# Seven half products in place of eight for the MLP input of two token blocks

## The chip, the cores and the metric

The kernel runs on one core of one Trainium2 chip. The metric is the device time of one execution in microseconds (us). Matmuls run on TensorE (PE in the profile), elementwise work on VectorE (DVE), ScalarE (ACT) and GpSimd (POOL); SyncE (SP) issues the transfers.

## The reference

Linear attention over 4 batches, 8 heads and 576 positions gives x of 2304 tokens by 512. A gated unit (GLU) and an MLP follow, both with float64 weights in memory and float32 results:

```
xn = x / rms(x) * rms_g
x2 = (silu(xn @ w_gate) * (xn @ w_val)) @ w_out      # 512 -> 1536 -> 512
h  = x2 @ w_in                                       # 512 -> 2048
out = silu(h) @ w_out2                               # 2048 -> 512
```

## The kernel before

Tokens are cut into five blocks: blocks 0 to 3 have 512 tokens, block 4 has 256. The 2048 MLP features are cut into 16 f groups of 128. Each float32 operand is kept as a high part (rounded to fp32r) and a low part (the rest), and each product is three matmuls: high by high, high by low, low by high (`PASS`).

For a block and an f group the input product (`part`, L250) is 12 matmuls: 4 chunks of 128 input features by 3 passes. ScalarE applies SiLU (L284) and makes the high part of h (L243), VectorE makes the low part (L244). The output product (`g2_mlp`, L337) takes all f groups of a sweep: for each tile of 128 tokens, 3 matmuls for each f group into one PSUM bank of the pool `ps_y`, which VectorE then adds to the block's sum in SBUF (L348; in the first sweep ScalarE copies, L346).

The MLP goes in six sweeps over all tokens, of 3, 3, 3, 3, 2 and 2 f groups. The order of the work is the order in which the code emits it, engine by engine. `stream` walks sweeps and blocks. A block's output product is not emitted at once: it waits in `pend` and is emitted after the SiLU and the split of a later input product, so that other matmuls lie between a SiLU and the products that read its result.

Weights of the next sweep are prepared in between. `stream` yields the PE time of each step; when W_PACE (5.5 us) or W_RUSH (3.2) has come together, `prep.tick` emits one step for up to three weights: the load (SP), the decode of the float64 words (five VectorE instructions, L154 to L165, then two GpSimd additions, L168), the high part (ACT, L191) and the low part (DVE, L194). Each engine works through its own queue in this order.

In the GLU the last sweep (two f groups) leaves each block's result in `ya` and splits it into `xs` (L317, L294), the MLP's input.

Of the kernel before, what the change touches and what calls it, by code (L numbers as in the profile page):

```python
# [20 lines left out]
def kernel(  # L21
# [99 lines left out]
    def wrows(w, f):  # L121
        return w.bitcast(U32)[f * P:(f + 1) * P, :]
# [139 lines left out]
    def g1_glu(f, j, hs, mid):  # L262
        prep.need((1, "g", f))
        p = ps_tile("ps_g", [P, blocks[j]])
        yield from proj(wt[1, "g", f], j, p)
        s = pools["s"][0].tile([P, blocks[j]], F32, tag="s", name="s", bufs=pools["s"][1])
        nc.scalar.activation(out=s, in_=p, func=AF.Silu)  # L267
        if blocks[j] == TB * P:
            yield from mid
        prep.need((1, "v", f))  # L270
        p = ps_tile("ps_g", [P, blocks[j]])
        yield from proj(wt[1, "v", f], j, p)
        nc.vector.tensor_tensor(out=s, in0=s, in1=p, op=ALU.mult)  # L273
        hs[f] = split_h(s, j)
        if blocks[j] < TB * P:
            yield from mid

    def g1_mlp(f, j, hs, mid, late):
        prep.need((2, "i", f))
        p = ps_tile("ps_g", [P, blocks[j]])  # L280
        yield from proj(wt[2, "i", f], j, p)
        yield from late
        s = pools["s"][0].tile([P, blocks[j]], F32, tag="s", name="s", bufs=pools["s"][1])
        nc.scalar.activation(out=s, in_=p, func=AF.Silu)  # L284
        hs[f] = split_h(s, j)
        yield from mid

    def g2_glu(fs, j, hs, first, last):
        prep.need(*[(1, "o", f) for f in fs])
        y = ya[j].rearrange("p (c t) -> p c t", c=KC)  # L290
        nn = 3 * len(fs)

        def low(d):
            nc.vector.tensor_tensor(  # L294
                out=xs[j][:, 1, d, :], in0=y[:, d, :],
                in1=xs[j][:, 0, d, :].bitcast(F32), op=ALU.subtract,
            )
# [57 lines left out]
    n2 = len(sweeps) - 1  # L355

    def stream():
        pend = ()
        prepped = 1
        for si, (kind, fs, side) in enumerate(sweeps):  # L360
            for j in range(NB) if si < n2 else [*range(NE), *range(NB - 1, NE - 1, -1)]:
                if si == 0 and j < NE:
                    continue
                hs = {}
                end = si == n2 and j == NE
                for f in fs:
                    if kind == 1:
                        yield from g1_glu(f, j, hs, pend)
                        pend = ()
                    else:  # L370
                        short = blocks[j] < TB * P
                        keep = f == fs[0] and (end or short)
                        mid, late_mid = ((), pend) if short else (pend, ())
                        yield from g1_mlp(f, j, hs, *(((), ()) if keep else (mid, late_mid)))
                        if not keep:
                            pend = ()
                    if si and prepped == si and si + 1 < len(sweeps):
                        prep.jobs += prep_list(si + 1)
                        prepped += 1
                if kind == 1:  # L380
                    pend = g2_glu(fs, j, hs, si == 0, si == n1)
                else:
                    pend = g2_mlp(fs, j, hs, si == n1 + 1, si == n2, end)
        yield from pend
# [699 lines left out]
    with tc.manual_schedule():  # L1084
# [105 lines left out]
```

## Time and profile before

| | us |
|---|---|
| median of 3 runs (lowest to highest) | 971.16 (970.67 to 972.09) |
| the profiled execution, and its span | 969.33, 967.5 |
| PE busy over the span | 961.1 (99%) |
| DVE, ACT, POOL busy | 558.1 (58%), 385.9 (40%), 292.1 (30%) |
| chain that ended last, PE's share | 97% |
| L250, input products: busy, count | 467.9, 2256 |
| L337, MLP output products: busy, count | 200.8, 870 |

The MLP takes the span from about 575 us to the end. A row of a timeline gives the start of a piece of work and how long it took; the bracket tells how long its engine had been idle, and what ended that.

### The profile page before, as it was taken

What the parts mean: (1) busy time and instruction counts of PE and PEld (TensorE: products, weight loads), DVE (VectorE), ACT (ScalarE), POOL (GpSimd) and SP (SyncE); (2) the same over time, 40 slices, a digit from 0 to 9 for tenths busy, and PEclk for the clock granted to TensorE, in tenths of its full rate; (3) what the DMA queues carried; (4) which work ended last, traced back from release to release, by engine and by line L of the source; (5) the groups of instructions that cost most, each with busy time, mean ns of one, the idle gap of its engine ahead of it and who ended that gap; (6) DMA issues with size and microseconds to landing.
All of it is one profiled execution on the core that took longest, in us unless ns stands there. A gap on an engine that the chain in (4) does not pass through costs nothing.

```text
span 967.5 us, 16801 instructions
## 1 busy us (share of the span) xinstructions
PE 961.1 (99%) x6658; PEld 807.8 (83%) x6658; DVE 558.1 (58%) x1163; ACT 385.9 (40%) x891; POOL 292.1 (30%) x308
## 2 busy tenths in 40 slices
PE   8999999999999999999999999999999999999998
PEld 6888888888889888888888888888888888888887
DVE  6998999685533466763326764515635635435634
ACT  6999886643211134331113344433223223222221
POOL 8888656253300133431002313403302402102200
PEclk9999999999999999999999999999999999999999
DMA  8655544122200012220000211201201201100023
GB/s 193 168 134 135 143 130 116 66 88 65 66 1 1 6 61 66 88 87 22 0 1 22 66 44 45 88 1 44 87 1 43 66 22 44 44 1 23 22 87 109
DMA packets 79486, 60.39 MB, mean 62 GB/s; under 512 B 27312, under 2 KB 73648, under 8 KB 79408
## 3 DMA queue, kind: packets, MB, share of 16 engines
q1 hardware_dynamic: 79136, 59.26, 21.2%
q8 instruction: 52, 0.85, 0.4%
q14 instruction: 26, 0.21, 0.1%
q10 hardware_dynamic: 272, 0.07, 0.0%
HBM read 49.87 MB, written 4.72 MB: 56 GB/s over the span
## 4 chain that ended last, share of the span: by engine, by line
PE 97%; DVE 1%; ACT 1%; issue 0%; DVEq 0%
PE g L250 47%; PE y L337 20%; PE y L304 13%; PE b L661 4%; PE b L250 4%; PE b L845 2%; PE kv L741 2%; PE b L1061 2%; PE b L634 2%; PE b L941 1%; PE b L821 1%; PE b L1102 0%; ACT e L710 0%; DVE small L678 0%; ACT m L176 0%; DVE m L154 0%
## 5 line engine op out<-in xcount | busy, mean ns | idle before, releaser
L250 PE MATMUL g<-xs,w 128*128 128x512 f32 (+1 forms) x2256 | 467.9, 366 | 0.0
L250 PEld LDWEIGHTS g<-xs,w 128*128 128x128 f32 x2256 | 391.1, 188 | 70.2
L168 POOL TENSOR_TENSOR m<-m,raw 128x512 int32<-128x512 int32 x136 | 188.5, 1386 | 581.3 <-issue 415.2
L244 DVE TENSOR_TENSOR h<-s,h 128x512 fp32r<-128x512 f32 (+1 forms) x134 | 96.0, 717 | 185.2 <-ACT h L243 185.2
L337 PE MATMUL y<-w,h 128*128 128x512 f32 (+1 forms) x870 | 200.8, 388 | 0.0
L337 PEld LDWEIGHTS y<-w,h 128*128 128x128 f32 x870 | 162.2, 188 | 33.3
L243 ACT ACTIVATE h<-s 128x512 fp32r<-128x512 f32 (+1 forms) x134 | 78.9, 589 | 182.0 <-DVE s L273 160.0
L304 PE MATMUL y<-h,w 128*128 128x512 f32 (+1 forms) x648 | 135.5, 366 | 0.2 <-DVE h L244 0.2
L304 PEld LDWEIGHTS y<-h,w 128*128 128x128 f32 x648 | 112.2, 189 | 20.2 <-DVE h L244 0.4
L284 ACT ACTIVATE s<-g 128x512 f32<-128x512 f32 (+1 forms) x80 | 44.5, 556 | 170.8 <-PE g L250 170.3
L348 DVE TENSOR_TENSOR ya<-y,ya 128x512 f32<-128x512 f32 (+1 forms) x91 | 62.2, 684 | 57.8 <-PE y L337 56.5
L315 DVE TENSOR_TENSOR ya<-y,ya 128x512 f32<-128x512 f32 (+1 forms) x80 | 50.4, 636 | 58.2 <-PE y L304 58.0
L273 DVE TENSOR_TENSOR s<-s,g 128x512 f32<-128x512 f32 (+1 forms) x54 | 33.9, 627 | 82.6 <-PE g L250 81.6
L710 ACT ACTIVATE e<-b,nb 128x128 f32<-128x128 f32 x272 | 76.2, 428 | 7.6 <-issue 4.4
L191 ACT ACTIVATE w<-m 128x512 fp32r<-128x512 f32 x68 | 43.3, 636 | 68.1 <-POOL m L168 67.6
L678 DVE TENSOR_REDUCE small<-b 128x4 f32<-128x512 f32 (+1 forms) x80 | 51.4, 643 | 6.5 <-PE b L661 2.7
L267 ACT ACTIVATE s<-g 128x512 f32<-128x512 f32 (+1 forms) x54 | 29.6, 548 | 59.9 <-PE g L250 59.8
L194 DVE TENSOR_TENSOR w<-m,w 128x512 fp32r<-128x512 f32 x68 | 51.2, 754 | 0.1
L587 POOL TENSOR_TENSOR sq<-sq 128x256 f32<-128x256 f32 (+1 forms) x80 | 45.4, 577 | 3.5
L661 PE MATMUL b<-om,hl 64*64 64x128 f32 x1152 | 41.9, 276 | 1.2 <-ACT hl L649 1.0
L583 POOL TENSOR_TENSOR sq<-x 128x512 f32<-128x512 f32 (+1 forms) x40 | 39.1, 980 | 12.9 <-DVE ns L596 4.7
L661 PEld LDWEIGHTS b<-om,hl 64*64 64x64 f32 x1152 | 32.1, 132 | 8.9 <-issue 3.6
(72 smaller groups left out, 703.7 us busy)
## 6 DMA issues: line engine op xcount, KB each, us to landing
raw<-in_moe_w_out_dram SPq DMA_DIRECT2D x28, 512.0 KB, 3.6
raw<-in_moe_w_in_dram SPq DMA_DIRECT2D x16, 512.0 KB, 3.7
raw<-in_moe_w_gate_dram SPq DMA_DIRECT2D x12, 512.0 KB, 3.7
raw<-in_moe_w_val_dram SPq DMA_DIRECT2D x12, 512.0 KB, 3.6
qT<-e SPq DMA_DIRECT2D x72, 64.0 KB, 2.6
x<-in_k_dram SPq DMA_DIRECT2D x16, 256.0 KB, 3.5
x<-in_q_dram SPq DMA_DIRECT2D x16, 256.0 KB, 3.3
va<-in_v_dram SPq DMA_DIRECT2D x32, 128.0 KB, 4.3
```

Of the source, the lines that this page charges most:

```text
L168: tt(out=mi, in0=mi, in1=(low if step == 5 else high).bitcast(I32), op=ALU.add)
L194: nc.vector.tensor_tensor(out=st.t[:, 1, :], in0=st.m.bitcast(F32), in1=st.t[:, 0, :].bitcast(F32), op=ALU.subtract)
L243: nc.scalar.activation(out=ht[:, 0, :], in_=s, func=AF.Copy)
L244: nc.vector.tensor_tensor(out=ht[:, 1, :], in0=s, in1=ht[:, 0, :].bitcast(F32), op=ALU.subtract)
L250: nc.tensor.matmul(out=ps, lhsT=w[:, a, cc * P:(cc + 1) * P], rhs=xs[j][:, c, cc, :], start=(n == 0), stop=(n == 3 * KC - 1),)
L304: nc.tensor.matmul(out=ps, lhsT=wt[1, "o", f][:, a, d * P:(d + 1) * P], rhs=hs[f][:, c, :], start=(n == 0), stop=(n == nn - 1),)
L315: nc.vector.tensor_tensor(out=y[:, d, :], in0=ps, in1=y[:, d, :], op=ALU.add)
L337: nc.tensor.matmul(out=ps, lhsT=hs[f][:, a, t * P:(t + 1) * P], rhs=wt[2, "p", f][:, c, d0:d1], start=(n == 0), stop=(n == nn - 1),)
L348: nc.vector.tensor_tensor(out=o[:, t, d0:d1], in0=ps, in1=o[:, t, d0:d1], op=ALU.add)
L661: nc.tensor.matmul(out=st.ps[e][cols, j, :], lhsT=st.xt[rows, j, cols], rhs=om2[rows, :], start=True, stop=True, skip_group_check=True,)
L678: nc.vector.tensor_reduce(out=st.mx.rearrange("p (j e) -> p e j", e=2)[:, e], in_=st.ps[e], axis=AX.X, op=ALU.max)
L710: nc.scalar.activation(out=st.e[r][:, :, h, :] if blocks4 else st.e[r][:, h, :], in_=src.rearrange("p (a f) -> p a f", a=4) if blocks4 els ...
```

## The change

For blocks 0 and 1 and a pair of f groups, the input product is a 2 by 2 product of halves: two blocks by two halves of the 512 input features (call block 0's halves a0 and b0, block 1's a1 and b1), times two feature halves by two f groups. It is eight half products of 6 matmuls. Strassen's scheme in Winograd's form needs seven, with sums of tokens and of weights as operands. All MLP sweeps now have two f groups, so there are eight.

- `token_sums`, once, at the end of the GLU: four subtractions of 128x1024 on GpSimd, in place in `ya` of blocks 0 and 1, and each result split into high (ACT) and low (DVE).
- `Mlp`, in place of `prep` for the MLP's weights: twelve jobs a sweep, one at a time, whenever M_PACE (3.6 us of PE) has come together. It adds two sums of weights for each sweep (four GpSimd instructions of 128x256, L444), and splits each (L426 on ACT, L430 on DVE).
- `quad`: the seven products P1 to P7 in four PSUM banks pa, pe, pb, pc. Partial sums pass from bank to bank by three ScalarE copies (L513), one of them, e, to SBUF; VectorE adds e to pb and later to pc (L525, `both`). pb is added to by P3, P5 and P6, and read in between. Between the products stand up to six tiles of the output product of blocks 3 and 4 of the sweep before (`more`), called Y1 to Y6 here. In the first sweep two matmuls initialise pb and pc.
- In blocks 2 and on the order is: input of block 2, first f, output of block 0; input of block 2, second f, output of block 1; then blocks 3 and 4.

```diff
-    for i, n in enumerate([3, 3, 3, 3, 2, 2]):
+    for i, n in enumerate([2] * (NF2 // 2)):
...
+        return [                                  # token_sums
+            lambda: less(a1, a1, a0),
+            lambda: (high(1, a1), less(b1, b1, a1)),
+            lambda: low(1, a1),
+            lambda: (high(2, b1), less(a0, b1, a0)),
...
+            self.jobs += [                        # Mlp.plan
+                (("load", s), lambda: load("i", 0)),
+                (("load", s), lambda: (dec("i", 0), load("i", 1))),
+                (("load", s), lambda: (hi("i", 0), dec("i", 1), load("p", 0))),
+                (("load", s), lambda: (lo("i", 0), hi("i", 1), load("p", 1))),
+                (("load", s), lambda: (lo("i", 1), sum12())),
+                (("s", s), lambda: (shi(0), sum34())),
+                (("s", s), lambda: slo(0)),
+                (("s2", s), lambda: (shi(1), dec("p", 0))),
+                (("s2", s), lambda: (slo(1), hi("p", 0))),
+                (("s2", s), lambda: (lo("p", 0), dec("p", 1))),
+                (("p", s), lambda: hi("p", 1)),
+                (("p", s), lambda: lo("p", 1)),
+            ]
...
+        product(w1, 0, half(0, 0), pa, True)      # quad: P1
+        copy(pb, pa)
+        yield from more()
...
+        product(s12, 0, summ(1), pe, True)        # P2
+        copy(e, pe)
+        yield from more()
+        yield step
+        product(s12, KH, summ(2), pb, False)      # P3
+        copy(pc, pb)
+        yield from more()
+        yield step
+        product(w1, KH, half(0, KH), pa, False)   # P4
+        t = silu(pa, s_tile())
+        yield from more()
+        hs[0][f1] = split_h(t, 0)
...
+        product(s34, 0, summ(3), pb, False)       # P5
+        t = both(pb)
+        yield from more()
+        hs[1][f2] = split_h(t, 1)
+        yield step
+        product(w2, KH, summ(4), pb, False)       # P6
+        t = silu(pb, s_tile())
+        yield from more()
...
+        product(s34, KH, half(1, KH), pc, False)  # P7
+        hs[1][f1] = split_h(both(pc), 1)
...
+            yield from quad(s, iter(pend), hs)    # stream
...
+            for n, f in enumerate(fs):
+                yield from g1_mlp(f, 2, hs[2], (), out_of(n, hs[n]))
...
+            elif due > M_PACE and mlp.tick():
                 due = 0.0
```

**Place 1: pb between P5 and P6, TensorE.** What TensorE does, before, in the second sweep (w0_0 to w0_2 are input weights; g is a PSUM bank of an input product, y one of an output tile, h the split result of a SiLU):

```order
L250 MATMUL g_7345<-xs0_90,w0_1_6987 128x512 x12
L250 MATMUL g_7365<-xs0_90,w0_2_7033 128x512 x12
L250 MATMUL g_7383<-xs1_91,w0_0_6910 128x512 x12
L337 MATMUL y_7401<-w0_3_7083,h_7320 128x512 [waits Activation_49]
L337 MATMUL y_7401<-w0_3_7083,h_7320 128x512
L337 MATMUL y_7401<-w0_3_7083,h_7320 128x512 [waits DVE_49]
```

In the changed kernel, third sweep (g_7485 is pb, y_7583 is Y5; w1_5 and w1_6, w1_7 and w1_8 hold token sums):

```order
L501 MATMUL g_7485<-w1_5_6531,w0_0_7503 128x512 [waits Activation_49]
L501 MATMUL g_7485<-w1_6_6532,w0_0_7503 128x512
L501 MATMUL g_7485<-w1_5_6531,w0_0_7503 128x512 [waits DVE_49]
L501 MATMUL g_7485<-w1_5_6531,w0_0_7503 128x512
L501 MATMUL g_7485<-w1_6_6532,w0_0_7503 128x512
L501 MATMUL g_7485<-w1_5_6531,w0_0_7503 128x512
L340 MATMUL y_7583<-w0_3_7142,h_7462 128x512 x3
L340 MATMUL y_7583<-w0_1_7226,h_7480 128x512 x3
L501 MATMUL g_7485<-w1_7_6556,w1_1_7361 128x512 [waits DVE_49]
L501 MATMUL g_7485<-w1_8_6557,w1_1_7361 128x512
L501 MATMUL g_7485<-w1_7_6556,w1_1_7361 128x512 x2
```

Before, the input products follow each other without a wait, each in a bank of its own. Now P6 adds to the bank of P5, and its first matmul waits for VectorE, with the six matmuls of Y5 between the two.

**The same place, VectorE.** What VectorE does, before, around a decode in the same sweep (ya0 is the sum of block 0):

```order
L348 TENSOR_TENSOR ya0_95<-y_7401,ya0_95 128x512
L154 TENSOR_SCALAR m0_7412<-raw0_7346 128x512
L157 TENSOR_SCALAR raw0_7346<-raw0_7346 128x512
L160 TENSOR_SCALAR m0_7412<-m0_7412 128x512
L162 TENSOR_SCALAR raw0_7346<-raw0_7346 128x512
L165 TENSOR_SCALAR m0_7412<-m0_7412 128x512
L348 TENSOR_TENSOR ya0_95<-y_7422,ya0_95 128x512
L348 TENSOR_TENSOR ya0_95<-y_7433,ya0_95 128x512
L348 TENSOR_TENSOR ya0_95<-y_7444,ya0_95 128x512
```

In the changed kernel, from the eviction of Y4 (y_7554) to that of Y5; m1 and raw1 are the decode of an output weight, w0_2 a weight that is split, s_7580 the sum of pb (g_7485) and e:

```order
L351 TENSOR_TENSOR ya3_3690<-y_7554,ya3_3690 128x512
L430 TENSOR_TENSOR w0_2_7529<-m0_7505,w0_2_7529 128x512
L154 TENSOR_SCALAR m1_7563<-raw1_7363 128x512
L157 TENSOR_SCALAR raw1_7363<-raw1_7363 128x512
L160 TENSOR_SCALAR m1_7563<-m1_7563 128x512
L162 TENSOR_SCALAR raw1_7363<-raw1_7363 128x512
L165 TENSOR_SCALAR m1_7563<-m1_7563 128x512
L244 TENSOR_TENSOR h_7571<-s_7552,h_7571 128x512
L525 TENSOR_TENSOR s_7580<-g_7485,e_7487 128x512
L351 TENSOR_TENSOR ya4_3691<-y_7583,ya4_3691 128x512
```

The eviction of Y4, the low part of one weight, the whole decode of the next and a split of h stand ahead of the addition L525 that reads pb. In sweeps 3 to 8 these rows are alike; in sweep 2 ScalarE evicts Y4, and in sweep 1 there is no Y5.

**Place 2: the second h of block 2, ScalarE.** What ScalarE does, before, where it makes two weights' high parts (L191):

```order
L191 ACTIVATE w1_4_7681<-m0_7613 128x512
L191 ACTIVATE w1_5_7715<-m1_7683 128x512
L284 ACTIVATE s_7729<-g_7713 128x512
L243 ACTIVATE h_7731<-s_7729 128x512
L284 ACTIVATE s_7747<-g_7734 128x512
L243 ACTIVATE h_7749<-s_7747 128x512
```

In the changed kernel, after the output of block 0 (w0_4 and w0_5 are the next sweep's input weights, s_7752 and h_7754 the second f group of block 2):

```order
L426 ACTIVATE w0_4_7711<-m0_7675 128x512
L426 ACTIVATE w0_5_7748<-m1_7713 128x512
L284 ACTIVATE s_7752<-g_7690 128x512
L243 ACTIVATE h_7754<-s_7752 128x512
L284 ACTIVATE s_7770<-g_7757 128x512
L243 ACTIVATE h_7772<-s_7770 128x512
```

Two high parts stand ahead of a SiLU in both. Before, TensorE has 12 matmuls of 512 columns, 24 of 256 and three more between that SiLU's product (g_7713) and the first matmul that reads h_7731. Now block 1's output product follows g_7690, the jobs that end in the two high parts are emitted within it, and from its end there are the 12 matmuls of g_7757 and three more up to the first that reads h_7754.

## Rows read from the trace of the kernel before

**Rows 1.** The page: busy time by engine, then the chain of waits by engine
```profile
PE 961.1 (99%) x6658; PEld 807.8 (83%) x6658; DVE 558.1 (58%) x1163; ACT 385.9 (40%) x891; POOL 292.1 (30%) x308
...
PE 97%; DVE 1%; ACT 1%; issue 0%; DVEq 0%
```

**Rows 2.** Busy time by stretch, in the MLP: us, PE, PEld, DVE, ACT, POOL, PEclk
```profile
700.00:760.00 60.00, 60.00 (x283) 50.36 (x282) 27.06 (x50) 16.47 (x29) 10.91 (x8) 1.00 0.11 34
...
577.00:968.00 391.00, 387.19 (x1805) 324.25 (x1803) 181.89 (x326) 115.74 (x202) 73.40 (x52) 1.00 0.14 45
```

**Rows 3.** Timeline of TensorE, MLP outputs: start us, us, engine line op out<-in xcount
```profile
852.02 6.32 PE L337 MATMUL y<-w,h 128*128 128x512 f32 x27
```

**Rows 4.** Timeline of VectorE, same stretch: evictions of these outputs
```profile
854.29 0.69 DVE L348 TENSOR_TENSOR ya<-y,ya 128x512 f32<-128x512 f32 x1 [2.20 <-PE y L337]
856.33 0.69 DVE L348 TENSOR_TENSOR ya<-y,ya 128x512 f32<-128x512 f32 x1 [1.35 <-PE y L337]
858.37 0.69 DVE L348 TENSOR_TENSOR ya<-y,ya 128x512 f32<-128x512 f32 x1 [1.35 <-PE y L337]
```

**Rows 5.** Timeline of VectorE, MLP: a decode and what follows it
```profile
897.12 0.42 DVE L165 TENSOR_SCALAR m<-m 128x512 uint32<-128x512 uint32 x1
897.46 0.69 DVE L244 TENSOR_TENSOR h<-s,h 128x512 fp32r<-128x512 f32 x1
898.06 1.28 DVE L348 TENSOR_TENSOR ya<-y,ya 128x512 f32<-128x512 f32 x2
...
901.31 0.69 DVE L348 TENSOR_TENSOR ya<-y,ya 128x512 f32<-128x512 f32 x1 [0.67 <-PE y L337]
901.91 0.68 DVE L194 TENSOR_TENSOR w<-m,w 128x512 fp32r<-128x512 f32 x1
902.63 0.43 DVE L154 TENSOR_SCALAR m<-raw 128x512 uint32<-128x512 uint32 x1
...
903.98 0.42 DVE L165 TENSOR_SCALAR m<-m 128x512 uint32<-128x512 uint32 x1
```

**Rows 6.** Timeline of GpSimd, same stretch
```profile
891.57 2.70 POOL L168 TENSOR_TENSOR m<-m,raw 128x512 int32<-128x512 int32 x2 [6.82 <-issue]
897.68 3.02 POOL L168 TENSOR_TENSOR m<-m,raw 128x512 int32<-128x512 int32 x2 [3.41 <-ACT h L243]
```

**Rows 7.** Timeline of VectorE, a decode beside GpSimd
```profile
603.46 1.42 DVE L154 TENSOR_SCALAR m<-raw 128x512 uint32<-128x512 uint32 x1
604.80 1.53 DVE L157 TENSOR_SCALAR raw<-raw 128x512 uint32<-128x512 uint32 x1
606.25 0.41 DVE L160 TENSOR_SCALAR m<-m 128x512 f32<-128x512 f32 x1
```

**Rows 8.** Timeline of GpSimd, same stretch
```profile
602.96 3.08 POOL L168 TENSOR_TENSOR m<-m,raw 128x512 int32<-128x512 int32 x2 [10.30 <-DVE m L165]
```

**Rows 9.** Timeline, all engines: a wait of TensorE in the GLU
```profile
198.72 2.69 POOL L168 TENSOR_TENSOR m<-m,raw 128x512 int32<-128x512 int32 x2 [1.43 <-ACT m L176]
...
200.49 1.21 DVE L244 TENSOR_TENSOR h<-s,h 128x256 fp32r<-128x256 f32 x1 [0.48 <-ACT h L243]
...
201.75 0.98 PE L304 MATMUL y<-h,w 128*128 128x256 f32 x6 [0.22 <-DVE h L244]
```

**Rows 10.** Timeline of ScalarE, MLP: SiLU and high half
```profile
874.11 0.60 ACT L284 ACTIVATE s<-g 128x512 f32<-128x512 f32 x1 [1.46 <-PE g L250]
874.74 0.63 ACT L243 ACTIVATE h<-s 128x512 fp32r<-128x512 f32 x1
```

**Rows 11.** Groups by line in the MLP: busy us, mean ns, idle before
```profile
L191 ACT ACTIVATE w<-m 128x512 fp32r<-128x512 f32 x20 | 12.6, 629 | 50.1 <-POOL m L168 50.1
```

**Rows 12.** Timeline, 256-column evictions at the end of the GLU
```profile
575.06 0.42 ACT L317 ACTIVATE xs<-ya 128x256 fp32r<-128x256 f32 x1 [0.25 <-DVE ya L315]
575.27 0.42 DVE L315 TENSOR_TENSOR ya<-y,ya 128x256 f32<-128x256 f32 x1
```

**Rows 13.** Timeline of TensorE, the start of the program
```profile
1.44 2.50 PE L1102 MATMUL b<-zero 128*128 128x512 f32 x5 [1.44 <-DVE mhalf L1090]
```

More of the change, by code (lines that the diff above doesn't have):

```diff
@@ L278, in g1_mlp @@
     def g1_mlp(f, j, hs, mid, late):
-        prep.need((2, "i", f))
-        p = ps_tile("ps_g", [P, blocks[j]])
+        mlp.need((2, "i", f))
+        p = ps_tile("ps_g" if blocks[j] == TB * P else "ps_y", [P, blocks[j]])
         yield from proj(wt[2, "i", f], j, p)
@@ L291, in g2_glu @@
         nn = 3 * len(fs)
+        keep = KC // 2 if j == 1 else 0
         def low(d):
@@ L315, in g2_glu @@
                 nc.vector.tensor_tensor(out=y[:, d, :], in0=ps, in1=y[:, d, :], op=ALU.add)
-            if last:
+            if last and d >= keep:
                 nc.scalar.activation(out=xs[j][:, 0, d, :], in_=y[:, d, :], func=AF.Copy)
-                if d:
+                if d > keep:
                     low(d - 1)
@@ L322, in g2_glu @@
             low(KC - 1)
+        if last and j == 1:
+            sums.extend(token_sums())
     def g2_mlp(fs, j, hs, first, last, end):
-        prep.need(*[(2, "p", f) for f in fs])
+        mlp.need(*[(2, "p", f) for f in fs])
         nt = blocks[j] // P
@@ L355, with w_tile, token_sums, less @@
     n2 = len(sweeps) - 1
+    KH = KC // 2
+    tok, sums = {}, []
+    def w_tile(side, slot):
+        pool = pools["w"][2] if side and slot < W_EARLY else pools["w"][side]
+        return pool.tile([P, 2 * KC * P], F32R, tag=f"w{side}_{slot}", name=f"w{side}_{slot}")
+    def token_sums():
+        y0, y1 = (ya[j].rearrange("p (c t) -> p c t", c=KC) for j in (0, 1))
+        a0, b0, a1, b1 = y0[:, :KH], y0[:, KH:], y1[:, :KH], y1[:, KH:]
+        def less(out, x, y):
+            nc.gpsimd.tensor_tensor(out=out, in0=x, in1=y, op=ALU.subtract)
+        def high(n, x):
+            if n == 1:
+                tok[n] = [xs[1][:, a, :KH, :] for a in range(2)]
+            else:
+                tok[n] = [
+                    w_tile(1, 3 + 2 * (n - 2) + a).rearrange("p (c t) -> p c t", c=KH) for a in range(2)
+                ]
+            nc.scalar.activation(out=tok[n][0], in_=x, func=AF.Copy)
+        def low(n, x):
+            nc.vector.tensor_tensor(out=tok[n][1], in0=x, in1=tok[n][0].bitcast(F32), op=ALU.subtract)
+        return [
[3 more added lines that the diff above has]
+            lambda: (high(2, b1), less(a0, b1, a0)),
+            lambda: low(2, b1),
+            lambda: (high(3, a0), less(b0, b0, b1)),
+            lambda: low(3, a0),
+            lambda: high(4, b0),
+            lambda: low(4, b0),
+        ]
@@ L359, in stream @@
         prepped = 1
-        for si, (kind, fs, side) in enumerate(sweeps):
-            for j in range(NB) if si < n2 else [*range(NE), *range(NB - 1, NE - 1, -1)]:
+        for si, (kind, fs, side) in enumerate(sweeps[:n1 + 1]):
+            for j in range(NB):
                 if si == 0 and j < NE:
@@ L364, in stream @@
                 hs = {}
-                end = si == n2 and j == NE
                 for f in fs:
[L367 to L377, printed above, removed]
+                    yield from g1_glu(f, j, hs, pend)
@@ L378, in stream @@
+                    pend = ()
+                    if si and prepped == si and si < n1:
                         prep.jobs += prep_list(si + 1)
                         prepped += 1
[L380 to L384, printed above, removed]
+                pend = g2_glu(fs, j, hs, si == 0, si == n1)
+                if si == n1 and j == 0:
+                    mlp.mark(("load", 0))
+                    mlp.mark(("s", 0))
+                    mlp.plan(0)
@@ new lines, in stream @@
+        ns = len(sweeps) - n1 - 1
+        mlp.mark(("s2", 0))
+        for s in range(ns):
+            fs = [2 * s, 2 * s + 1]
+            first, last = s == 0, s == ns - 1
+            out_of = lambda j, h, end=False: g2_mlp(fs, j, h, first, last, end)
+            while sums:
+                sums.pop(0)()
+            hs = {}
+            yield from quad(s, iter(pend), hs)
+            if not last:
+                mlp.plan(s + 1)
+                for m in ("load", "s", "s2"):
+                    mlp.mark((m, s + 1))
+            hs[2] = {}
+            for n, f in enumerate(fs):
+                yield from g1_mlp(f, 2, hs[2], (), out_of(n, hs[n]))
+            pend = out_of(2, hs[2])
+            hs[3], hs[4] = {}, {}
+            if last:
+                yield from g1_mlp(fs[0], 4, hs[4], (), ())
+                yield from g1_mlp(fs[1], 4, hs[4], (), pend)
+                yield from g1_mlp(fs[0], 3, hs[3], (), ())
+                yield from g1_mlp(fs[1], 3, hs[3], out_of(4, hs[4]), ())
+                yield from out_of(3, hs[3], True)
+            else:
+                yield from g1_mlp(fs[0], 3, hs[3], pend, ())
+                yield from g1_mlp(fs[1], 3, hs[3], (), ())
+                for f in fs:
+                    yield from g1_mlp(f, 4, hs[4], (), ())
+                pend = chain_of(out_of(3, hs[3]), out_of(4, hs[4]))
@@ L387, with chain_of @@
+    def chain_of(*its):
+        for it in its:
+            yield from it
     class Op:
@@ L1156 @@
             due += c
-            if due > (W_PACE if prep.done(1) else W_RUSH):
-                prep.tick()
+            if sums:
+                sums.pop(0)()
+            elif prep.jobs or prep.pipe:
+                if due > (W_PACE if prep.done(1) else W_RUSH):
+                    prep.tick()
+                    due = 0.0
+            elif due > M_PACE and mlp.tick():
                 due = 0.0
```

117 lines of the change are left out of this document (116 added, 1 removed).

## Prediction

> **What bounds the kernel now.** I read the page first: PE is busy for 99% of the span, and the chain that ended last is PE for 97% [rows 1]. Then the busy time by stretch: in the middle of the MLP PE is busy for 60.00 of 60 us, while DVE, ACT and POOL are at 27.06, 16.47 and 10.91 [rows 2]. So the MLP costs its matmuls and nothing else, and whatever takes matmuls away gains unless PE has to wait where it did not. Their pitch comes from the evictions: three matmuls for each of three f groups fill a tile, and the evictions start 2.04 us apart [rows 4], 0.227 us for each matmul of 512 columns (27 matmuls in 6.32 us [rows 3] say the same). I call six of them, 1.36 us, a unit: each of P1 to P7 is one, so is each of Y1 to Y6 (from the second sweep on), and an input product of a whole block is two.
>
> **What is saved.** For each pair of f groups, 42 matmuls in place of 48, eight times: 48 x 0.227 = 10.9 us. The two that initialise banks give back 0.45. The output product has as many matmuls as before. With no wait of PE the profiled 969.33 us would become 958.9.
>
> **Latencies.** From the issue of the last matmul of a tile to its eviction 0.23 us: 852.02 [rows 3] plus nine pitches is 854.06, the eviction starts at 854.29 [rows 4]. From the end of a VectorE instruction to the matmul that waited for it 0.05 us (200.49 + 1.21 against 201.75 [rows 9]). A VectorE instruction of 512 columns runs 0.69 us, but the next one starts 0.60 after it (897.46 to 898.06, 901.31 to 901.91 [rows 5]); a split's low part holds the next decode back 0.72 (901.91 to 902.63); the five decode instructions start within 1.35 (902.63 to 903.98), and the next follows 0.34 after the fifth (897.12 to 897.46).
>
> **Place 1, the wait of P6 for VectorE (sweeps 3 to 8).** The first matmul of P6 can't issue before L525 has read pb. Ahead of L525 in VectorE's queue stands the eviction of Y4, which can't start before Y4 ends. From that end: 0.23 to the eviction, 0.60 to the low part of a weight, 0.72 to the decode, 1.35 within it, 0.34 to the split of h, 0.60 to L525, 0.69 for it, 0.05 back to PE: 4.58 us. L525 itself is priced by the eviction rows, which also read a PSUM bank and an SBUF tile; its other condition, the end of P5, comes far earlier. PE has P5 and Y5 in that time, 2 x 1.36 = 2.72. PE waits 1.86 us, six times: 11.2 us. Bounds: 1.5 each if the eviction starts at once, the decode follows the split at 0.60 and the hand-over is free; 3.2 if the split of the weight is caught by a GpSimd addition (1.35, half the pair of [rows 6]; [rows 9] show a split of h, 256 wide, that took 1.21 so). I take 1.86, since by my order GpSimd's last work before that point, the additions of the decode before, is over when Y4 ends.
>
> In sweep 2 ScalarE evicts the Y tiles, so the decode runs early; there L525 comes after ScalarE's eviction of Y4 and h's high part: 0.23 + 0.63 + 0.63, then 0.60 + 0.69 + 0.10 = 2.9 against 2.72: 0.2 to 0.3 us. I take 0.3.
>
> In sweep 1 the Y tiles are the GLU's block 4, half as wide, and there are only four. P6 follows P5 at once, so the cover is one unit. From the end of Y4: 0.23, an eviction of 0.42, ScalarE's copy of 0.42 [rows 12], the high part of h 0.63 [rows 10] (0.13 for the hand-overs), then 0.60 for the low part, 0.72 + 1.35 + 0.34 for split and decode, and 0.69 + 0.05 for L525: 5.6 less 1.36, a wait of 4.2. The matmul that initialises pc waits for the GLU's last product to be read (0.23 + 0.42 + 0.05, less one pitch: 0.5), and the first output tile may wait 0.3 for its weight's low part. Sweep 1 together: 5.0 us, 3 to 6.5.
>
> **Place 2, h of block 2's second f (sweeps 2 to 7).** Time zero is the end of block 0's output. VectorE evicts at 0.23, decodes the first weight of the next sweep and ends at 0.83 + 1.35 + 0.42 = 2.60; GpSimd's two additions follow at 2.74 and take 3.02 when a split of h comes right behind the decode (897.12, 897.46 and 897.68 [rows 5, 6]), to 5.76. The second decode is emitted behind block 1's first tile: 2.72 + 1.36 + 0.23 + 0.60 = 4.91. That is within GpSimd's second addition. Decode instructions that start there wait: with GpSimd's pair at 602.96 to 606.04 [rows 8], L154 took 1.42 and L157 1.53 in place of 0.42 [rows 7]. So L154 runs from about 5.63, the decode ends at 7.40, GpSimd's pair (2.70 when left alone [rows 6]) goes from 7.54 to 10.24. ScalarE now makes the high part of that weight (0.63 [rows 11]), and only then the SiLU and the high part of h (0.63 each from start to start [rows 10]): 10.29 + 1.89 = 12.18. PE ends the input product of block 3 at 4 x 1.36 + 2 x 1.36 + 2.72 = 10.88, has three matmuls more, and wants h at 11.56: it waits 0.67 for the high part, and some 0.3 more for the low part (0.69 + 0.05, two matmuls between). 0.95 x 6 = 5.7 us. Bounds: 0.2 if L154 is not caught (all 1.1 earlier), 2.3 if L157 is caught too, as in rows 7. I take 0.95, the plain order of these rows.
>
> **What costs nothing.** ScalarE's three copies and the two weight splits a sweep: at 16.47 of 60 us it has room, and each copy has at least two units before its reader. The 36 more evictions and the splits on VectorE lie beside matmuls outside the two places. The four subtractions and their splits at the GLU's end have blocks 2 to 4 of its last sweep as cover, some 40 us; by the decode additions (1.35 for 512 columns [rows 6]) they take about 11 us of GpSimd. Without that cover P2 or P3 would wait once, for a few us. The loads are as many and as large as before.
>
> **The sum.** -10.9 + 0.45 + 5.0 + 0.3 + 11.2 + 5.7 = +11.8 us; 969.33 becomes 981.1. The median of the runs is 1.83 us above the profiled one, so 982.9 is the forecast.
>
> **The rivals.**
> 1. The cover suffices and PE waits nowhere for long: 971.16 - 10.4 = 960.7 us. For it: VectorE is busy less than half of the MLP [rows 2]. Against it: the order is fixed, and between the end of Y4 and L525 VectorE has 4.3 us of its own work whatever its mean load. 8%.
> 2. Place 1 as worked out, place 2 nearly without a wait (0.2 each): 978. For it: there the result hangs on one instruction being caught by GpSimd. 25%.
> 3. More is caught: the second decode meets both GpSimd additions (2.3 at place 2), which puts 8 us more on the forecast: 991. It is the far slower side of the same mechanism, and decides if VectorE comes to that decode before GpSimd's second addition starts, 0.5 us earlier than by my sum. 12%.
> 4. The waits lower TensorE's clock. Granted in this trace is 1.00, which is 2.4 GHz, in every stretch of the MLP, where PE never waits [rows 2]; the program's first five matmuls, after 1.44 us of idle time, took 2.50 us [rows 13], (2.50 - 0.63)/4 = 0.47 apart, twice the later pitch and so as at 1.2 GHz. If each of 13 waits cost one unit at that pitch, 13 x 6 x 0.24 = 19 us more: 1002. No row shows a fall behind a wait; the longest wait that I expect is 4.2 us, once, and the others are under 3. 3%. The Trainium skill, "TensorE: Matmul & The Clock Gate", Part 1 on the clock gate, has an idle TensorE fall back to half its clock: by that the waits would cost more than they last. The start of this trace agrees with half a clock after idle time (0.47 us).
> 5. Both places at their lower bounds (1.5 and 0.2; sweep 1 at 3): -10.9 + 0.45 + 3 + 9 + 1.2 = +2.8 at most, less if the covers hold a little longer: no change to be measured, or little. 7%.
>
> **Chances and range.** My forecast has 45%. Runs of the kernel before lie within 0.15% of their median, so 0.2% (2 us) is about what can be told from no change: faster is below 969.2, slower above 973.1. Faster: rival 1 and a little of 5, 10%. Same: the rest of 5 and the low end of 2, 7%. Slower: 83%. The range must hold the forecast, rival 2 and some of 3 and 5: 973 to 990. The likeliest case alone gives 979 to 986.
>
> **What would show it.** In the changed profile PE should be some 10 us less busy in matmuls but idle for over 20 us in the MLP; the wait list should name L501 waiting for DVE L525, about seven times at 1.5 to 2.2 us and once at about 4, and L340 waiting for ACT L243 or DVE L244 about six times. VectorE should show a decode between the eviction of Y4 and L525. I am wrong if PE stays at 60 of 60 us in the MLP, if L525 starts right at the end of P5, or if the largest waits have another releaser.

## The result and the profile after

The changed kernel takes 986.38 us (median; 984.07 to 986.96) against 971.54 for the kernel before: a ratio of the means of 1.0149, with a 95% interval from 1.0131 to 1.0167. The forecast was 982.9, a loss of 11.8 us; the loss is 14.8. So the direction and most of the size came out, and the time is 3.5 us above the forecast. The profiled execution took 986.49 us with a span of 984.3.

The page of the kernel after, busy time by engine and the chain by engine, to be read against [rows 1]:

```profile
PE 960.4 (98%) x6612; PEld 799.7 (81%) x6612; DVE 610.8 (62%) x1233; ACT 409.6 (42%) x933; POOL 329.6 (33%) x344
...
PE 85%; DVE 6%; POOL 3%; ACT 3%; issue 2%; DMA 1%; SPq 0%; DVEq 0%; POOLq 0%
```

There are 46 matmuls fewer, and the chain now runs over DVE, POOL and ACT for 12% of the span. PE's busy time hardly fell, though 46 matmuls are worth 10.4 us: the records count a matmul behind a wait, or at the lower clock, longer. In the kernel e9 below, with the same 6612 matmuls and almost no wait, PE is busy for 952.0.

The middle of the MLP, busy time by engine, to be read against [rows 2]:

```profile
700.00:760.00 60.00, 58.14 (x265) 47.62 (x264) 39.72 (x70) 18.13 (x32) 21.26 (x17) 1.00 0.15 45
```

PE was at 60.00 here and waits now. What it waits for, from 205 us on (us in total, times, longest):

```profile
PE g L501 <- DVE s L525: 13.0, 7, 3.7
PE y L340 <- ACT h L243: 2.0, 6, 0.3
PE y L305 <- ACT h L243: 0.5, 1, 0.5
PE y L305 <- DVE h L244: 0.2, 1, 0.2
```

The first two are place 1 and place 2 of the prediction. The list counts idle time only. From start to start of the matmuls, less the pitch of 0.227, place 1 loses 1.82 us in each of sweeps 3 to 8 (gaps of 1.93 and 0.34), and place 2 loses 0.87 in each of six sweeps (0.71, 0.34, 0.39 and 0.34), though the list gives it 0.3.

Place 1 in the third sweep, all engines (start, length, engine and line, idle time before it and what ended that):

```profile
681.61 0.69 DVE L351 TENSOR_TENSOR ya<-y,ya 128x512 f32<-128x512 f32 x1 [2.03 <-PE y L340]
682.22 0.68 DVE L430 TENSOR_TENSOR w<-m,w 128x512 fp32r<-128x512 f32 x1
682.77 1.52 PE L340 MATMUL y<-w,h 128*128 128x512 f32 x6
682.82 0.42 DVE L154 TENSOR_SCALAR m<-raw 128x512 uint32<-128x512 uint32 x1
...
684.49 0.69 DVE L244 TENSOR_TENSOR h<-s,h 128x512 fp32r<-128x512 f32 x1
...
685.10 0.69 DVE L525 TENSOR_TENSOR s<-g,e 128x512 f32<-128x512 f32 x1
...
685.84 1.66 PE L501 MATMUL g<-w,w 128*128 128x512 f32 x6 [1.54 <-DVE s L525]
```

The steps stand 0.61, 0.60, 1.67, 0.61 and 0.74 apart, and Y5 (682.77) is the only cover behind P5: the chain of [rows 4, 5], each step within 0.12 of its price.

Place 2 in the same sweep, all engines:

```profile
700.91 3.02 POOL L168 TENSOR_TENSOR m<-m,raw 128x512 int32<-128x512 int32 x2 [13.18 <-issue]
...
703.10 1.12 DVE L154 TENSOR_SCALAR m<-raw 128x512 uint32<-128x512 uint32 x1
...
705.69 2.69 POOL L168 TENSOR_TENSOR m<-m,raw 128x512 int32<-128x512 int32 x2 [1.76 <-issue]
...
708.41 0.63 ACT L426 ACTIVATE w<-m 128x512 fp32r<-128x512 f32 x1 [3.81 <-POOL m L168]
...
708.95 0.58 ACT L284 ACTIVATE s<-g 128x512 f32<-128x512 f32 x1
...
709.56 0.63 ACT L243 ACTIVATE h<-s 128x512 fp32r<-128x512 f32 x1
...
710.25 1.94 PE L340 MATMUL y<-w,h 128*128 128x512 f32 x6 [0.32 <-ACT h L243]
```

L154 was caught by GpSimd, that is, it took longer beside GpSimd's additions (1.12 in place of 0.42, as in [rows 7]); the weight's high part L426 follows GpSimd's pair, the SiLU and h follow that, and PE follows h.

In the first sweep, VectorE and TensorE around L525:

```profile
583.09 0.68 DVE L430 TENSOR_TENSOR w<-m,w 128x512 fp32r<-128x512 f32 x1
583.69 0.42 DVE L154 TENSOR_SCALAR m<-raw 128x512 uint32<-128x512 uint32 x1
...
585.37 0.68 DVE L525 TENSOR_TENSOR s<-g,e 128x512 f32<-128x512 f32 x1
...
586.10 2.92 PE L501 MATMUL g<-w,w 128*128 128x512 f32 x6 [3.71 <-DVE s L525]
...
588.83 2.76 PE L501 MATMUL g<-xs,w 128*128 128x512 f32 x6
```

Six matmuls behind the wait took 2.7 us in place of 1.36: 13 of them are about 0.43 apart. The busy table of that stretch gives the granted clock, third number from the end, as 0.50, that is 1.2 GHz:

```profile
585.90:592.00 6.10, 5.90 (x14) 4.64 (x15) 3.76 (x5) 3.01 (x5) 2.33 (x2) 0.50 0.28 86
```

And at the end of the GLU, where no wait was foreseen:

```profile
525.96 3.02 POOL L168 TENSOR_TENSOR m<-m,raw 128x512 int32<-128x512 int32 x2 [2.36 <-issue]
...
527.74 1.79 DVE L430 TENSOR_TENSOR w<-m,w 128x512 fp32r<-128x512 f32 x1
...
529.45 0.68 DVE L273 TENSOR_TENSOR s<-s,g 128x512 f32<-128x512 f32 x1
...
530.84 0.50 PE L305 MATMUL y<-h,w 128*128 128x512 f32 x1 [0.50 <-ACT h L243]
531.57 3.72 PE L305 MATMUL y<-h,w 128*128 128x512 f32 x15 [0.22 <-DVE h L244]
```

The low part of the first input weight was caught by GpSimd (1.79 in place of 0.68) and stood ahead of the gate's product L273, from which h is made; PE lost 1.3 us in the gaps of 0.89, 0.73 and 0.34.

### The profile page after: what moved, and what is told of

Read it like the earlier page. It is cut to its first block, busy times and chain, and to the rows that moved or that the text cites. A ratio compares the mean times of both kernels' runs of the same rounds, so it can differ in the third digit from the quotient of the medians.

```text
span 984.3 us, 16831 instructions
## 1 busy us (share of the span) xinstructions
PE 960.4 (98%) x6612; PEld 799.7 (81%) x6612; DVE 610.8 (62%) x1233; ACT 409.6 (42%) x933; POOL 329.6 (33%) x344
## 4 chain that ended last, share of the span: by engine, by line
PE 85%; DVE 6%; POOL 3%; ACT 3%; issue 2%; DMA 1%; SPq 0%; DVEq 0%; POOLq 0%
PE g L250 32%; PE y L340 17%; PE y L305 13%; PE g L501 7%; PE b L906 3%; PE y L250 2%; PE b L250 2%; POOL m L168 2%; PE b L1090 2%; PE kv L986 2%; PE b L879 2%; PE b L1306 1%; PE b L1066 1%; DVE m L154 1%; ACT w L426 1%
## 5 line engine op out<-in xcount | busy, mean ns | idle before, releaser
L168 POOL TENSOR_TENSOR m<-m,raw 128x512 int32<-128x512 int32 x136 | 189.2, 1391 | 548.4 <-issue 433.0
L250 PE MATMUL g<-xs,w 128*128 128x512 f32 (+1 forms) x1680 | 358.6, 371 | 0.0
L250 PEld LDWEIGHTS g<-xs,w 128*128 128x128 f32 x1680 | 296.1, 188 | 54.9
L340 PE MATMUL y<-w,h 128*128 128x512 f32 (+1 forms) x870 | 210.4, 389 | 2.0 <-ACT h L243 2.0
L340 PEld LDWEIGHTS y<-w,h 128*128 128x128 f32 x870 | 161.6, 188 | 40.1 <-ACT h L243 4.5
L244 DVE TENSOR_TENSOR h<-s,h 128x512 fp32r<-128x512 f32 (+1 forms) x134 | 93.3, 696 | 116.9 <-ACT h L243 116.9
L305 PE MATMUL y<-h,w 128*128 128x512 f32 (+1 forms) x648 | 136.7, 366 | 0.9 <-ACT h L243 0.5
L351 DVE TENSOR_TENSOR ya<-y,ya 128x512 f32<-128x512 f32 (+1 forms) x127 | 85.9, 684 | 76.9 <-PE y L340 76.7
L305 PEld LDWEIGHTS y<-h,w 128*128 128x128 f32 x648 | 112.5, 188 | 22.1 <-DVE h L244 1.2
L316 DVE TENSOR_TENSOR ya<-y,ya 128x512 f32<-128x512 f32 (+1 forms) x80 | 50.5, 636 | 64.6 <-PE y L305 64.3
L273 DVE TENSOR_TENSOR s<-s,g 128x512 f32<-128x512 f32 (+1 forms) x54 | 33.8, 626 | 80.7 <-PE g L250 79.7
L426 ACT ACTIVATE w<-m 128x512 fp32r<-128x512 f32 x40 | 25.1, 627 | 81.6 <-POOL m L168 81.5
L267 ACT ACTIVATE s<-g 128x512 f32<-128x512 f32 (+1 forms) x54 | 29.5, 547 | 60.2 <-PE g L250 59.8
L501 PE MATMUL g<-w,w 128*128 128x512 f32 x144 | 38.9, 407 | 13.0 <-DVE s L525 13.0
L501 PE MATMUL g<-xs,w 128*128 128x512 f32 x192 | 50.3, 398 | 0.0
L501 PEld LDWEIGHTS g<-w,w 128*128 128x128 f32 x144 | 27.0, 193 | 21.4 <-DVE s L525 16.2
```

What stands on the lines that cost most here:

```text
L168: tt(out=mi, in0=mi, in1=(low if step == 5 else high).bitcast(I32), op=ALU.add)
L244: nc.vector.tensor_tensor(out=ht[:, 1, :], in0=s, in1=ht[:, 0, :].bitcast(F32), op=ALU.subtract)
L250: nc.tensor.matmul(out=ps, lhsT=w[:, a, cc * P:(cc + 1) * P], rhs=xs[j][:, c, cc, :], start=(n == 0), stop=(n == 3 * KC - 1),)
L305: nc.tensor.matmul(out=ps, lhsT=wt[1, "o", f][:, a, d * P:(d + 1) * P], rhs=hs[f][:, c, :], start=(n == 0), stop=(n == nn - 1),)
L340: nc.tensor.matmul(out=ps, lhsT=hs[f][:, a, t * P:(t + 1) * P], rhs=wt[2, "p", f][:, c, d0:d1], start=(n == 0), stop=(n == nn - 1),)
L501: nc.tensor.matmul(out=ps, lhsT=w[:, a, (c0 + c) * P:(c0 + c + 1) * P], rhs=x(b, c), start=(start and n == 0), stop=(n == 3 * KH - 1), ski ...
```

## The experiments

The theory: TensorE waits because jobs of the weights stand ahead of L525 on VectorE (place 1) and ahead of the SiLU on ScalarE (place 2). The rivals: the hand-over of the bank costs this by itself; the eight sweeps cost it; the waits only move when the jobs do; TensorE's clock adds to them.

In e1, e2 and e3 a job that comes due inside a marked stretch is noted and emitted at `release()`; `left` says which job, by the number of jobs that are left.

**e1, L525 ahead of the job.**

```diff
-        t = silu(pa, s_tile())
+        t, mlp.left = silu(pa, s_tile()), 3       # P4
...
         t = both(pb)
-        yield from more()
+        yield from (release(), more())[1]         # P5
```

> The changed kernel, with one job of the weights (low part of one output weight, decode of the next) emitted behind L525 instead of between the evictions of Y4 and L525, in every sweep; all work is kept. Theory (P6 waits because that job stands ahead of L525 on VectorE): the six waits of about 1.8 us in sweeps 3 to 8 go (-10.9), the wait of 3.7 us in sweep 1 shrinks to about 1.4 (-2.3), and the 13 matmuls at half pitch behind it go as well if it was the length of the wait that lowered the clock (-2.7): 986.4 becomes 970.5, or 973.2 if the clock still falls. Rival 1 (the hand-over of pb costs this whatever stands ahead): the waits stay, 986. Rival 2 (the job, emitted later, makes the second output weight late): the L501 waits go and L340 waits 1 to 2 us in each sweep for DVE L430 instead: 977 to 981.

Measured: 973.73 us (973.16 to 975.56), 12.65 less. All that is left of place 1 in the list of waits is one in the first sweep; new beside it are two waits for the second output weight (L430 and L426):

```profile
PE y L340 <- DVE w L430: 2.0, 1, 2.0
PE y L340 <- ACT h L243: 1.9, 6, 0.3
...
PE g L501 <- DVE s L525: 1.4, 1, 1.4
...
PE y L340 <- ACT w L426: 0.6, 1, 0.6
```

So the hand-over of the bank is not what costs, and the job is. The wait of 1.4 us lowered no clock: the matmuls behind it are 0.34 and then 0.23 apart. Of the 3.2 us that are missing to 970.5, 3.1 are the second rival, in the first sweep alone: the output weight decoded later makes L340 wait, in three gaps (0.98, 2.51 and 0.33).

**e2, h ahead of the job.**

```diff
             for n, f in enumerate(fs):
-                yield from g1_mlp(f, 2, hs[2], (), out_of(n, hs[n]))
-            pend = out_of(2, hs[2])
+                yield from (setattr(mlp, "left", (None, 9)[n]), g1_mlp(f, 2, hs[2], (), out_of(n, hs[n])))[1]
+            pend = (release(), out_of(2, hs[2]))[1]
```

> The changed kernel, with one job of the weights (low part of the first input weight, high part of the second) emitted behind the SiLU and the split of block 2's second f instead of ahead of them, in every sweep but the last; all work is kept. Theory (ScalarE's high part of that weight, which waits for GpSimd, stands ahead of the SiLU): L340's waits for ACT L243 (six places, 0.87 us of gaps each) go: -5.2, 986.4 becomes 981.2. Rival (the h buffer comes free late, or VectorE's evictions of block 1's output hold the low part): the waits stay, 986. Second rival: the sums of weights come later and P2 waits for them: 984 to 988, with L501 waiting for DVE L430.

Measured: 980.53 us (979.82 to 981.35), 5.85 less, and no wait of L340 is left in its list. The edit is worth far more than the 2.0 us that the list had given these waits: the gaps (5.2) were the measure. In this profile 8 matmuls in place of 13 ran slowly behind the first sweep's wait; that is 1.0 us of the 6.5 by which the two profiled executions differ (986.49 and 980.03), and not due to the edit.

**e3, both.** The diffs of e1 and e2 together.

> Both edits together, all work is kept. If the two places are independent the gains add: 986.4 - 10.9 - 5.0 (sweep 1 with the clock) - 5.2 = 965.3, below the kernel before (971.5). If the two jobs run into each other in the same sweep, or the waits move on to other weights: 970 to 975.

Measured: 968.83 us (967.95 to 969.54), 17.55 less, against 18.5 for the two alone; a ratio of 0.9972 (0.9960 to 0.9985) to the kernel before. The two places are independent to within 1 us, and of the 3.5 us missing to 965.3, 3.2 are e1's new wait again (gaps of 1.00, 2.51 and 0.34).

**e5, the kernel before in eight sweeps.**

```diff
-    for i, n in enumerate([3, 3, 3, 3, 2, 2]):
+    for i, n in enumerate([2] * (NF2 // 2)):
```

> The kernel before with eight MLP sweeps of two f groups in place of 3, 3, 3, 3, 2 and 2, and nothing else: eight plain half products, the old preparation of weights. Theory (the sweeps cost nothing, since the two more evictions of each tile lie beside matmuls): 971.4, the same as before, so that all that the changed kernel loses comes from the combined products and the new order of the weights' jobs. Rival (shorter sweeps leave the preparation of weights too little time, and TensorE waits for them): 974 to 985, with L337 or L250 waiting for DVE L194.

Measured: 971.42 us, a ratio of 1.0002 (0.9993 to 1.0011). The sweeps cost nothing; that rival falls.

**e6, one job later at the end of the GLU.**

```diff
-            elif due > M_PACE and mlp.tick():
+            elif due > (M_PACE if tok or len(mlp.jobs) != 9 else 6) and mlp.tick():
```

> The changed kernel with one job of the first sweep's weights (low part of the first input weight, high part of the second), which falls into the GLU's last sweep, one step later; all work is kept. Theory (the low part, L430, which took 1.79 us beside GpSimd, stands ahead of the product L273 of the gate, and L305 waits for the h made from it): L305's waits for ACT L243 and DVE L244 at 530 to 532 us, 1.5 us in gaps, go: about 985 us. Rival (the crowd there comes from the low parts of x, L295, that took 3.20 for two): they stay: 986.4. Second rival: the following jobs come later and P2 waits for a sum of weights: 987 to 990.

Measured: 984.78 us (one run; its span 982.6 against 984.3). The gaps at 530 to 532 us are gone but for one of 0.34, so the job was their cause. But a wait for another split of h came at 547 us (gaps of 0.97 and 0.34): 0.9 of the 1.3 us moved on, as the rival has it that the waits only move. That split took 1.54 us in place of 0.69; it began at 545.84, beside a subtraction of the token sums (L372, two in 6.10 us from 540.73). Half of the 1.7 us of span is due to fewer slow matmuls in the first sweep (9 in place of 13).

**e7, both edits, e6, and a first sweep with its jobs sooner and its tiles one product later.**

```diff
         copy(pb, pa)
-        yield from more()
+        mlp.due = M_PACE if s else 1.9
+        yield from (more() if s else ())
```

> Both edits of e3 and the one of e6, and in the first sweep the jobs come sooner (every 1.9 us of PE's work in place of 3.6) and the four tiles of the GLU's block 4 stand behind P2, P3, P4 and P5 in place of P1 to P4; all work is kept. From e3's 968.8: the GLU's wait -1.5, the wait of P6 in the first sweep -1.5, L340's waits for the late output weight there -2.9: 962.9, where the 46 matmuls saved alone would give 971.4 - 10.4 = 961.0. Rival (the jobs sooner in the first sweep meet GpSimd or the low parts of x and hold the copies between the banks): 965 to 969.

Measured: 967.05 us (965.14 to 970.20): the expectation failed by 4.2, and the time is that of its rival. The waits for the late output weight went, but P6 still waited in the first sweep. GpSimd and VectorE there, then the wait:

```profile
580.75 2.71 POOL L168 TENSOR_TENSOR m<-m,raw 128x512 int32<-128x512 int32 x2 [3.20 <-issue]
580.87 1.46 DVE L295 TENSOR_TENSOR xs<-ya,xs 128x256 fp32r<-128x256 f32 x1
...
582.25 1.76 DVE L244 TENSOR_TENSOR h<-s,h 128x512 fp32r<-128x512 f32 x1
583.94 0.68 DVE L525 TENSOR_TENSOR s<-g,e 128x512 f32<-128x512 f32 x1
...
584.67 2.93 PE L501 MATMUL g<-w,w 128*128 128x512 f32 x6 [3.17 <-DVE s L525]
```

The decode, now earlier, starts GpSimd's additions right where a low part of x and the split of h stand ahead of L525, and both are caught (1.46 in place of 0.42, 1.76 in place of 0.69). It is the rival's meeting with GpSimd, but what it holds is L525 and not the copies.

**e9, L525 cleared.**

```diff
-                if d > keep:                      # g2_glu
+                if d > keep and j < NB - 1:
                     low(d - 1)
...
-        hs[0][f1] = split_h(t, 0)                 # quad, behind P4
+        hs[0][f1] = split_h(t, 0) if s else t
...
-        t = both(pb)                              # behind P5
+        t, hs[0][f1] = both(pb), hs[0][f1] if s else split_h(hs[0][f1], 0)
```

> The kernel e7 with two moves in the first sweep: the low parts of x of block 4 (L295, which took 1.46 us beside GpSimd) all behind the last tile, and the split L244 of P4's h, which took 1.76 us beside GpSimd, behind L525; all work is kept. Theory (in e7 these two stand ahead of L525, caught by GpSimd's additions, and P6 waited 3.2 us, with 8 matmuls at half pitch behind it): L525 follows the decode at about 581 us, P6 waits for nothing or some tenths, the clock stays: 967.05 - 3.2 - 1.5 = 962.4. Rival (L525 itself or the eviction ahead of it is caught by GpSimd in turn): a wait of 1 to 2 us stays, 964 to 965.

Measured: 963.49 us (962.36 to 964.21), a ratio of 0.9917 (0.9903 to 0.9931) to the kernel before and 1.1 above the 962.4 expected: the seven products do pay once what stands ahead of L525 and h no longer holds them up. P6's gaps in the first sweep are 0.38 and 0.34 now, with no slow matmul behind them. Busy time by engine on its page:

```profile
PE 952.0 (99%) x6612; PEld 799.1 (83%) x6612; DVE 618.9 (64%) x1233; ACT 410.5 (43%) x933; POOL 331.8 (35%) x344
```

The middle of the MLP:

```profile
700.00:760.00 60.00, 60.00 (x289) 50.62 (x288) 39.83 (x67) 21.55 (x39) 18.16 (x16) 1.00 0.14 45
```

What is left in its list of waits behind the first 200 us:

```profile
PE y L305 <- DVE h L244: 0.8, 2, 0.6
PE y L340 <- DVE w L430: 0.4, 1, 0.4
```

VectorE does the same work as in the changed kernel (39.83 of 60 us against 39.72); only its order differs, and PE is back at 60.00.

**e4, graded waits.** To see what a wait does to TensorE's clock.

```diff
-            nc.vector.tensor_tensor(out=t, in0=x, in1=e, op=ALU.add)
+            for _ in range(1 + ((0, 0, 0, 1, 2, 3, 4, 6)[s] if x is pb else 0)):
+                nc.vector.tensor_tensor(out=t, in0=pe if x is pb and _ < (0, 0, 0, 1, 2, 3, 4, 6)[s] else x, in1=e, op=ALU.add)
```

> The changed kernel with more VectorE additions (128x512, PSUM and SBUF in, their results overwritten) ahead of L525 in place 1: none more in sweep 3, then 1, 2, 3, 4 and 6 more in sweeps 4 to 8, 0.60 us each. The waits of P6 should be about 1.8, 2.4, 3.0, 3.6, 4.2 and 5.4 us. Theory (a wait lowers TensorE's clock only where it is about as long as the one of sweep 1, 3.7 us, behind which 13 matmuls ran 0.43 apart): the sum of the added waits is 9.6 us, and about 2.7 more for each of the two or three longest: 1001 to 1004 us, with a granted clock near 0.5 behind them. Rival 1 (the fall in sweep 1 has to do with what ran before it, the short gaps of the GLU's last block, and not with the wait): no fall anywhere in sweeps 3 to 8: 996. Rival 2 (each wait counts): a fall behind all six: 1009 or more.

Measured: 1004.27 us (one run). TensorE in the fourth and the fifth sweep (L526 is L525 here):

```profile
736.31 2.12 PE L501 MATMUL g<-w,w 128*128 128x512 f32 x6 [2.34 <-DVE s L526]
738.23 2.69 PE L340 MATMUL y<-w,h 128*128 128x512 f32 x6
...
789.88 1.66 PE L501 MATMUL g<-w,w 128*128 128x512 f32 x6 [3.06 <-DVE s L526]
791.38 1.54 PE L340 MATMUL y<-w,h 128*128 128x512 f32 x6
```

The busy table of 3 us behind each wait, with the granted clock as the third number from the end:

```profile
737.80:740.80 3.00, 3.00 (x9) 2.38 (x8) 0.51 (x1) 1.59 (x3) 0.00 (x0) 0.52 0.58 168
790.50:793.50 3.00, 3.00 (x15) 2.46 (x14) 1.23 (x2) 2.38 (x4) 0.00 (x0) 1.00 0.59 175
```

The clock fell behind the shorter of the two waits and not behind the longer. The time lies at the upper end of the first theory (1001 to 1004), but its border near 3.7 us does not hold; and since the clock fell behind four of the six waits of sweeps 3 to 8, neither rival holds.

**e10, the same, turned round.**

```diff
-            for _ in range(1 + ((0, 0, 0, 1, 2, 3, 4, 6)[s] if x is pb else 0)):
+            for _ in range(1 + ((0, 0, 0, 6, 4, 3, 2, 1)[s] if x is pb else 0)):
```

> The kernel e4 with the number of added VectorE instructions turned round: 6, 4, 3, 2 and 1 more in sweeps 4 to 8. In e4 the gaps of 2.73, 4.18, 4.90 and 6.36 us (sweeps 4, 6, 7, 8) were followed by 8 or more matmuls 0.43 us apart, the gap of 3.45 (sweep 5) and that of 1.93 (sweep 3) by none. If the length of the wait alone decides, with some 3 us as the border and 2.73 by chance beyond it, the first three or four of these waits are followed by a fall and the last is not: about 1003. If the place in the sweep order decides (the moment that the chip looks), sweep 5 shows none again, though its wait is 4.9 us, and sweep 8 one behind its 2.7 us: 1001 to 1004 as well, but at other places. The rows behind each wait tell the two apart, not the time.

Measured: 1005.29 us (one run). All five waits of sweeps 4 to 8 have slow matmuls behind them, also that of the fifth sweep, so the place in the order does not decide; and the gap of 3.46, which had none in e4, now has:

```profile
903.19 1.77 PE L501 MATMUL g<-w,w 128*128 128x512 f32 x6 [3.07 <-DVE s L526]
904.76 2.76 PE L340 MATMUL y<-w,h 128*128 128x512 f32 x6
```

**e8, the kernel before once more.**

> The kernel before, unchanged, for a second trace of its first 200 us, which are instruction by instruction the same in both kernels. If the 2.5 us that the changed kernel's profile shows more there (its products of the GLU's block 4 begin at 192.3 in place of 189.8) differ from execution to execution, this trace shows a value between or beyond: 189.8 to 193. If they come with the change (another place of the tiles or of the code), it shows 189.8 again.

Measured: 970.41 us; the output products that the expectation speaks of (L304; they are the GLU's of block 3, not of block 4) begin at 190.97, between the values. That alone does not settle it; where each trace falls behind, told below, tells more.

## Why the prediction came out as it did

| term, us | forecast | measured |
|---|---|---|
| matmuls saved, less two that initialise | -10.45 | -10.4 (46 x 0.227) |
| place 1, sweeps 3 to 8 | 11.2 | 10.9 (6 x 1.82) |
| sweep 2 | 0.3 | 0.1 |
| sweep 1 | 5.0 | 3.9 (a gap of 4.09) |
| the clock behind it | rival 4 | 2.6 (13 x 0.2) |
| place 2 | 5.7 | 5.2 (6 x 0.87) |
| GLU's end | nothing | 1.3 |
| first 200 us | nothing | 1.4 to 2.5 (against e8 and the kernel before) |
| sum | 11.8 | 15.0 to 16.1 |

The medians are 14.8 apart; the span of the profile is 16.8 above that of the profile before and 15.7 above that of e8, so some 0.7 us stand in no row. That the forecast came as near as 3.5 us is in part luck: the terms of the waits were 2.1 us too high together, which hides part of the 5.3 to 6.4 that stand in no term of its sum.

- Place 1 is right in mechanism and size, and shown: e1 removes it by moving one job, with all work kept. VectorE's mean load [rows 2] decides nothing here: in e9 it is the same as in the changed kernel (39.83 and 39.72 of 60 us), and TensorE is busy for the whole stretch.
- Place 2 is right too, shown by e2. It hung on one instruction caught by GpSimd, and it was caught.
- Sweep 1: the wait was forecast as 4.2 and is 3.9. The steps put at 0.5 for the initialising matmul and 0.3 for the first output tile show no gap.
- Of what the prediction put at nothing, one sentence failed: that the GLU's end has cover. It looked at the token sums; the wait came from a job of the first input weights in the same stretch, whose low part GpSimd caught ahead of L273. e6 showed it, and showed behind it that the token sums are not free either: with that job gone, L305 lost 0.9 us to a split that ran beside them.
- Rival 4 was given 3%, for 13 waits. It holds, for one: the longest wait lowered the clock and cost 2.6 us more in the profile of the changed kernel, where the rival had put 1.4 on each wait (8 or 9 slow matmuls behind the same wait in other profiles, 1.6 to 1.8). The Trainium skill, "TensorE: Matmul & The Clock Gate", Part 1, by which an idle TensorE falls back to half its clock, agrees with the 0.50 of that stretch. The six waits of 1.8 us lowered nothing.
- Two of the signs named beforehand came out otherwise: PE is only 0.7 us less busy in place of 10, since part of the lost time is counted as busy, and in the MLP, from 577 us on, it is idle for 18.2 us (3.3 before) in place of over 20. The waits' releasers are those named; L501 has 7 waits for L525 in place of about 8, and L340 has the 6 named.
- The saving itself is real and was hidden by waits: without them the same seven products give 963.49, 7.5 below the kernel before. The 10.4 alone would give 960.6 (970.98 in the runs beside e9, less 10.4); the first 200 us and the waits left in e9's list lie between.

## What to carry to other kernels

When a change makes one matmul wait for an elementwise result, add up what stands ahead of that result in its engine's queue between the last thing that the engine must wait for and it; the engine's mean load does not tell. Before giving up such a change, move the work of later stages behind the one instruction that TensorE waits for: here the order of a few jobs decided between 986 and 963 us with the same instructions. Measure waits by the starts of the matmuls, since the list of waits gave less than half of one of them.

## What the runs showed of the hardware

**The clock behind waits.** The gap is from start to start of the matmuls on either side of the wait; slow are those that follow more than 0.36 us apart, mostly 0.43.

| gap, us | where | slow matmuls behind it |
|---|---|---|
| 1.8 to 1.94 | 20 waits of place 1, two in the first sweep of e1 and e3 | 0 |
| 2.51 | e1, e3, the first output tile | 0, 0 |
| 2.73 | e4, e10 | 8, 7 |
| 3.45, 3.46 | e4, e10, e7 | 0, 7, 7 |
| 4.09 to 4.18 | five kernels, first sweep; e4, e10 | 8 to 13 |
| 4.90, 6.36 | e4, e10 | 8, 8; 11, 10 |

The rows are those behind the first 200 us. Not every gap of 2.5 to 3.5 us has slow matmuls behind it, and its length alone does not decide; each fall cost some 1.4 to 2.6 us on top of the wait. In 6 of the 15 falls the second matmul behind the wait still comes 0.34 or less after the first; in the other 9 it comes 0.40 to 0.59 after it. Within the first 200 us a shorter gap had a fall behind it: 2.05 us in e1, where TensorE waited for a transfer until 130.8, and the granted clock is 0.50 from 132.2 to 135.5.

**The first 200 us.** All instructions there stand in the same order in every kernel, but the GLU's output products of block 3 begin at 189.84, 190.97 and 189.78 in the kernel before, e8 and e5, and at 191.9 to 193.4 in the changed kernel and the eight made from it. Two parts lie in this, by the starts of the same matmuls. Up to 126 us the traces lie 0.0 to 2.1 us behind that of the kernel before, 1.3 in the changed kernel; the kernel before itself does as much in e8 (1.3). Between 126 and 138 us the changed kernel loses 1.2 us more and the eight made from it 1.4 to 3.5, while e5 and e8 lose nothing there. So this second part comes with the change. A transfer lands later there. Transfers between 122 and 134 us, KB each and median us to landing, of the kernel before:

```profile
x<-in_q_dram SPq DMA_DIRECT2D x1, 256.0 KB, 3.2
```

and of the changed kernel:

```profile
x<-in_q_dram SPq DMA_DIRECT2D x1, 256.0 KB, 4.0
```

It is 3.4 and 3.3 in e5 and e8, and 3.9 to 5.3 in the eight made from the changed kernel. Why it takes longer there stays open; no run tried it, and that it is the cause of the whole loss is not shown.

**VectorE beside GpSimd.** In e7's rows the two VectorE instructions that read and write SBUF alone ran 1.0 us longer beside L168. An addition that reads a PSUM bank, L525, did not, in e9:

```profile
581.19 2.68 POOL L168 TENSOR_TENSOR m<-m,raw 128x512 int32<-128x512 int32 x2 [3.20 <-issue]
581.30 0.68 DVE L525 TENSOR_TENSOR s<-g,e 128x512 f32<-128x512 f32 x1
```

Over all of e9 none of the 16 L525, the 127 evictions L351 and the 54 gate products L273, which all read PSUM, took longer than 0.69 us, while the splits L244, L430 and L295, which do not, took up to 1.80, 1.75 and 1.79. So in these traces the instruction that TensorE waits for could be left beside GpSimd's work, while those ahead of it could be caught there.
